# Second part of a fused kernel: its 36 token tiles in five chunks of 768 or 1024 tokens instead of six of 768

## The chip, the cores and the metric

One Trainium2 chip, one core. A time is what one execution takes on the device, in microseconds (us); a kernel's time is the median of its runs. The engines are named as the profile names them: PE (matrix products) with PEld (its weight loads), DVE (vector), ACT (scalar), POOL, and SP, which here issues every DMA.

## The reference

Three stages, all float32, on 8 sequences of 576 tokens with 512 features:

```
attention in blocks of 64 tokens, 8 heads of 64       -> x   (8, 576, 512)
h = relu(x @ w_in); gate = sigmoid(conv3(h))          -> x = (h * gate) @ w_out        (d_ff 1024)
u = x + real(fft over features of (fft over tokens))
un = (u - mean(u)) / sqrt(var(u) + 1e-6)
out = u + relu(un @ w_ch1) @ w_ch2                    w_ch1 (512, 2048), w_ch2 (2048, 512)
```

The last line, on 8 * 576 = 4608 tokens, is the second part of the kernel, and the change is in it.

## The kernel before

**Products in three passes.** Every float32 operand is split into a high and a low half: ACT copies it to the reduced format (L278), DVE subtracts that from the original (L279). A product then takes three matmuls: high by high, high by low, low by high.

**The second part** comes after the attention, the gated layer and the transforms, which end at about 630 us. The normalised rows u lie in DRAM as 36 tiles of 128 tokens. Both of its layers use a scheme of seven block products (B11, B21, T2, T1, T3, B22, T4) on sums of quarter blocks in place of eight: two row tiles that belong together (halves a = 0 and 1 of a chunk) are worked on at once, and the eighteen pairs of tiles are cut into NCH = 6 chunks of HT = 3 pairs, 768 tokens each.

**First layer, chunk by chunk.** `prep(c)` (L854) makes the operands of chunk c while chunk c - 1 is multiplied: per half it loads three tiles u (ring of three buffers), takes mean and variance (`stats`, L781: bn_stats, bn_aggr and a chain of small instructions once for the three), normalises (L801), transposes on PE (L806), copies from PSUM into buffers `raw` (L866), forms the sums (L818), and splits seven operands into the ring `sx` of seven pairs. A pair of `sx` comes free when the last group of the chunk before has used it. `gates` are products before which the loads of u are not issued: groups 3 and 5 for chunk 1, groups 1 and 3 for the later ones. `group(c, g)` (L884), eight per chunk, does the seven products of 128 hidden features by the chunk: six matmuls each (L904) whose moving operand has HTOK = 384 columns, HT tiles of one half. It then copies (L888), adds (L880), applies relu (L889) and stores four results m1, u2, u3, h21 to `h_scr` in DRAM (L929). m1, u2 and u3 have rings of two buffers each, h21 one.

**Beside it.** `load_tw` (L762) loads and splits the weight sums of layer one while chunk 0 runs and of layer two while the last chunk runs; `weight_sums_late` (L743) makes the sums of layer two, eight pieces, two in each of the chunks 1 to 4.

**Second layer.** `second(c, j)` (L933), one for each of the eighteen pairs, reads the four results back, splits them and multiplies (L971, 256 columns); this part is the same for any number of chunks but for where it finds its data.

**The order of the work** is written by a planner (`Plan.emit`, L151). Each operation has an engine, a cost and a due number `prio`; going through modelled time, the planner issues on each engine the ready operation with the lowest number. A chunk has 56 numbers, seven per group, whatever its width. A buffer's reuse, a gate and the landing of a DMA are dependencies in that model. The order so found is fixed: on the chip each engine, and SP's queue, takes its instructions in it. Among PSUM tiles, `x` is a ring of four in order and `o` four in any order.

Of the kernel before, what the change touches and what calls it, by code (L numbers as in the profile page):

```python
# [30 lines left out]
NCH2 = 18  # L31
FT2 = 16

NCH = 6
HT = 3
HTOK = 128 * HT
FG = 8

B11, B21, T2, T1, T3, T4, B22 = range(7)
CUTS = ((0, 1024), (1024, 1792))  # L40
# [182 lines left out]
def kernel(  # L223
# [19 lines left out]
    buf, op = plan.buf, plan.op  # L243
# [18 lines left out]

    u_scr = [[dram_buf(f"u_scr{i}{j}") for j in range(2)] for i in range(NCH2)]
    t_scr = [[dram_buf(f"t_scr{n}{g}", 1792) for g in range(FG)] for n in range(2)]
    first_scr = [dram_buf(f"first_scr{i}", 2 * HTOK) for i in range(7)]
    h_scr = [[dram_buf(f"h_scr{c}_{k}", FG * HTOK) for k in range(4)] for c in range(NCH)]

    def load(dst, src, nbytes, prio, r=(), after=()):
        return op("SP", 450, lambda: sp.dma_start(out=dst(), in_=src()), prio, r=r, w=[dst], after=after, nbytes=nbytes)
# [551 lines left out]
    first = []  # L821

    def stats_first(prios):
        first[:] = stats([lambda p, n=n: load_u(n, "w", "wide", 2, p - 4) for n in range(2 * HT)], "d", prios)

    def norm_first(j, prio):

        u = buf("w", "wide", 2, [128, 2, 512])
        for a in range(2):
            src = u_scr[(HT * a + j) // 2][(HT * a + j) % 2]  # L830
            op("SP", 450, lambda a=a, src=src: sp.dma_start(out=u()[:, a, :], in_=src()), prio - 6, r=[src], w=[u], nbytes=262144)
        for a in range(2):
            part = lambda t, a=a: t[:, a, :]
            tp = turned(u, *first, HT * a + j, prio, part)
            aop(512, lambda part=part, tp=tp: act.copy(out=part(u()), in_=tp().rearrange("p d n -> p (d n)")), prio, [tp], [u], True)
        s = buf("w", "wide", 2, [128, 4, 256])
        a11, a12, a21, a22 = (lambda a=a, k=k: u()[:, a, 256 * k:256 * k + 256] for a in range(2) for k in range(2))
        s1, s2, s3, s4 = (lambda k=k: s()[:, k, :] for k in range(4))
        tt(s1, a21, a22, ALU.add, 256, prio + 1, [u], [s])
        tt(s3, a11, a21, ALU.subtract, 256, prio + 1, [u], [s])  # L840
        tt(s2, s1, a11, ALU.subtract, 256, prio + 1, [u, s], [s])
        tt(s4, a12, s2, ALU.subtract, 256, prio + 1, [u, s], [s])
        two = lambda t: t.rearrange("p (d n) -> p d n", d=2)
        for i, x, b in ((A11, a11, u), (A12, a12, u), (A22, a22, u), (S1, s1, s), (S2, s2, s), (S3, s3, s), (S4, s4, s)):
            dst = first_scr[i]
            op("SP", 450, lambda x=x, dst=dst: sp.dma_start(out=two(dst())[:, :, 128 * j:128 * j + 128], in_=two(x())), prio + 1.5, r=[b], w=[dst], nbytes=131072)

    def prep_first(prio):
        for k, i in enumerate((A11, A12, S2, S1, S3, A22, S4)):
            s = buf("b", "raw", 6, [128, 2 * HTOK])  # L850
            load(s, first_scr[i], 1024 * HTOK, prio - 8 + k, r=[first_scr[i]])
            left((0, i), s, 2 * HTOK, prio + k, [128, 2 * HTOK], last_fold)

    def prep(c, prios, gates):  # L854

        raw = lambda: buf("b", "raw", 6, [128, 2, HTOK])
        blocks = []
        for a in range(2):
            ps = prios[HT * a:HT * a + HT]
            us = [load_u(2 * HT * c + HT * a + j, "e", "u", 3, p - 12, [gates[a]]) for j, p in enumerate(ps)]  # L860
            mv, r = stats(us, "b", ps)
            two = [raw(), raw()]
            for j, u in enumerate(us):
                tp = turned(u, mv, r, j, ps[-1])
                for k, b in enumerate(two):
                    aop(256, lambda j=j, k=k, b=b, tp=tp: act.copy(out=b()[:, :, 128 * j:128 * j + 128], in_=tp()[:, 2 * k:2 * k + 2, :]), ps[-1], [tp], [b], True)  # L866
            blocks += two
        a11, a12, a21, a22 = blocks
        s1, s2 = raw(), raw()
        n, p = 2 * HTOK, prios[-1]  # L870
        tt(s1, a21, a22, ALU.add, n, p, [a21, a22], [s1])
        tt(s2, s1, a11, ALU.subtract, n, p, [s1, a11], [s2])
        tt(a21, a11, a21, ALU.subtract, n, p, [a11, a21], [a21])
        for k, (i, x) in enumerate(((A11, a11), (A12, a12), (S2, s2), (S1, s1), (S3, a21), (A22, a22))):
            left((c, i), x, n, p + k, [128, 2, HTOK])
        tt(a12, a12, s2, ALU.subtract, n, p + 5, [a12, s2], [a12])
        left((c, S4), a12, n, p + 6, [128, 2, HTOK])

    def add_to(x, acc, n, prio, cut=lambda t: t):
        vop(n, lambda: dve.tensor_tensor(cut(x()), acc(), cut(x()), op=ALU.add), prio, [acc, x], [x])  # L880
# [1 line left out]


    def group(c, g, t):  # L884
        n = HTOK
        x1, x2 = (buf("ps", "x", 4, [128, n]) for _ in range(2))
        x3 = buf("ps", "o", 4, [128, n])
        copy = lambda x, acc, prio: aop(n, lambda: act.copy(out=x(), in_=acc()), prio, [acc], [x], True)  # L888
        relu = lambda x, acc, prio: aop(n, lambda: act.activation(out=x(), in_=acc(), func=ACT.Relu), prio, [acc], [x], acc is not x)  # L889

        def product(i, acc, prio, first=True):
            w, c0 = weight_of(0, g, i)
            x = sx[c, i]

            def unit():
                wh, wl, xh, xl = (a() for a in (*w, *x))
                if len(xh.shape) == 2:
                    xh, xl = (a.rearrange("p (a b) -> p a b", a=2) for a in (xh, xl))
                todo = []
                for k in range(2):  # L900
                    ws = slice(c0 + 128 * k, c0 + 128 * k + 128)
                    todo += [(wh[:, ws], xh[:, k, :]), (wh[:, ws], xl[:, k, :]), (wl[:, ws], xh[:, k, :])]
                for m, (a, b) in enumerate(todo):
                    pe.matmul(acc(), a, b, start=first and m == 0, stop=m == 5, skip_group_check=not first)  # L904

            return op("PE", mm_cost(n, passes=6), unit, prio, r=[*w, *x], w=[acc], after=() if c or g else last_d if i in (B11, B21) else last_s)

        m1, u2, u3, h21 = (buf("b", name, 1 if name == "h21" else 2, [128, n]) for name in ("m1", "u2", "u3", "h21"))
        begun = product(B11, x1, t)
        copy(m1, x1, t)  # L910
        product(B21, x3, t + 1)
        add_to(m1, x3, n, t + 1)
        relu(m1, m1, t + 1)
        product(T2, x1, t + 4, False)
        copy(u2, x1, t + 4)
        product(T1, x2, t + 5)
        product(T3, x1, t + 6, False)
        copy(u3, x1, t + 6)
        add_to(u3, x2, n, t + 6)
        relu(u3, u3, t + 6)  # L920
        product(T4, x1, t + 9, False)
        relu(h21, x1, t + 9)
        product(B22, x2, t + 10, False)
        add_to(u2, x2, n, t + 10)
        relu(u2, u2, t + 10)
        for k, (x, p) in enumerate(((m1, t + 2), (u2, t + 11), (h21, t + 10), (u3, t + 7))):
            dst = h_scr[c][k]
            to = lambda dst=dst: dst().rearrange("p (j g n) -> p j g n", j=HT, g=FG)[:, :, g, :]
            op("SP", 450, lambda x=x, to=to: sp.dma_start(out=to(), in_=x().rearrange("p (j n) -> p j n", j=HT)), p, r=[x], w=[dst], nbytes=512 * n)  # L929
        return begun  # L930


    def second(c, j, t, begin, end):  # L933
# [18 lines left out]
        tt(a12, a12, a11, ALU.subtract, n, t - 2, [a12, a11], [a12])  # L952
        make(S4, a12, 5)
        make(A22, a22, 6)
        us = [load_u(2 * HT * c + HT * a + j, "e", "u", 3, t - 4 + 3 * a) for a in range(2)]
        x1, x2, x3 = buf("ps", "x", 4, [128, 256]), buf("ps", "o", 4, [128, 256]), buf("ps", "o", 4, [128, 256])
        lo, hi = (lambda x: x[:, :256]), (lambda x: x[:, 256:])

# [14 lines left out]
            op("PE", mm_cost(256, passes=3 * len(gs)), unit, prio, r=[*x, *(a for w, _ in ws for a in w)], w=[acc])  # L973

        def store(a, prio, part=lambda x: x):
            m = 2 * HT * c + HT * a + j
            op("SP", 450, lambda: sp.dma_start(out=part(out[m // 2, :, m % 2, :]), in_=part(us[a]())), prio, r=[us[a]], nbytes=262144)

        accs = {B11: x1, B21: x3, T2: x1, T1: x2, T3: x1, B22: x2, T4: x1}
# [26 lines left out]
    for i in range(NH):  # L1006
# [4 lines left out]
        for f in range(FT):  # L1011
# [2 lines left out]
            while later and t + f >= FT + 9 * (FG - len(later)):  # L1014
                weight_sums(*later.pop(0), t + f + 8, [step])
            if t + f == 88:
                stats_first([88 + 2 * n for n in range(2 * HT)])
            if t + f in (103, 111, 119):
                norm_first((t + f - 103) // 8, t + f)
        if i == 0:  # L1020
# [36 lines left out]
    for c in range(NCH):  # L1057
        t = start + span * c
        begun = []
        for g in range(FG):  # L1060
            begun.append(group(c, g, t + 7 * g))
            if 1 <= c <= 4 and g in (0, 2):
                n = 2 * (c - 1) + g // 2
                weight_sums_late(n, rows(w_ch2)[n], t + 7 * g + 10)
        if c + 1 < NCH:
            prep(c + 1, [t + 7 * g for g in (2, 3, 4, 4, 5, 6)], [begun[g] for g in ((1, 3) if c else (3, 5))])
    t = start + span * NCH
    for g in range(FG):
        load_tw(1, g, [t - span + 7 * g + 8, t - span + 7 * g + 11])
    for c in range(NCH):  # L1070
        for j in range(HT):
            second(c, j, t + 7 * (HT * c + j), c + j == 0, c == NCH - 1 and j == HT - 1)

    with tc.manual_schedule():
        make_identity(nc, ident)
# [117 lines left out]
```

## Time and profile before

| | |
|---|---|
| runs, us | 1356.65, 1357.13, 1360.19; median 1357.13 |
| the profiled execution | 1356.65 us, its span 1356.6 us |
| PE busy | 1321.3 us (97%), 11376 matmuls |
| PEld, DVE, ACT, POOL busy | 1291.2 (95%), 1047.4 (77%), 802.3 (59%), 73.0 us (5%) |
| DMA | 206.5 MB, mean 152 GB/s |
| mean granted clock of PE | 0.996 of full speed |
| chain that ended last | PE 52% of the span: L904 25%, L971 26% |

Busy time of PE is the union of spans whose ends are modelled, so matmuls overlap in it: what one matmul takes in a stream is read from the distance of their starts, not from their duration. The page's 40 slices show PE at nine tenths or more in all but the first two. The second part is the stretch from 612 us to the end.

### The profile page before, as it was taken

How to read it: one execution, taken by the hardware profiler on the slowest of the kernel's cores; microseconds unless marked ns; L12 is line 12 of the kernel's file. 1: busy time of each engine (PE TensorE's matmuls, PEld its weight loads, DVE VectorE, ACT ScalarE, POOL GpSimd, SP SyncE). 2: the span in 40 equal slices, each digit the busy share in tenths (PEclk: the TensorE clock that was granted, in tenths of full speed). 3: DMA queues.
4: the chain of work that ended last, by engine and by line, in shares of the span. 5: the costliest groups of instructions: out<-in, count | busy, mean ns of one | idle time of the engine just before them, and what ended most of it. 6: DMA issues, size and time to landing. Idle time of an engine off the chain costs nothing.

```text
span 1356.6 us, 29701 instructions
## 1 busy us (share of the span) xinstructions
PE 1321.3 (97%) x11376; PEld 1291.2 (95%) x11376; DVE 1047.4 (77%) x2027; ACT 802.3 (59%) x2189; POOL 73.0 (5%) x195
## 2 busy tenths in 40 slices
PE   6899999999999999998999999999999999999999
PEld 4699999999999999997999999999999999999998
DVE  7999898889977686767776676765598777777773
ACT  6777675868677676655766665656763333333331
POOL 1101020101011110210000000000000000000000
PEclk9999999999999999999999999999999999999999
DMA  8523514232522132236856657669855554554441
GB/s 308 157 86 116 185 64 151 83 123 89 190 88 81 61 111 63 63 112 199 251 178 186 198 165 230 184 194 298 243 161 187 169 172 134 164 171 142 154 141 39
DMA packets 154573, 206.50 MB, mean 152 GB/s; under 512 B 11584, under 2 KB 103360, under 8 KB 154432
## 3 DMA queue, kind: packets, MB, share of 16 engines
q1 hardware_dynamic: 154432, 204.61, 48.0%
q8 instruction: 89, 1.46, 0.5%
q14 instruction: 52, 0.43, 0.1%
HBM read 130.51 MB, written 74.06 MB: 151 GB/s over the span
## 4 chain that ended last, share of the span: by engine, by line
PE 52%; DVE 1%; ACT 0%; issue 0%; DMA 0%; DVEq 0%; ACTq 0%
PE x L904 21%; PE x L971 15%; PE o L971 11%; PE o L904 4%; PE o L806 1%; DVE sxl L279 0%; DVE raw L818 0%; DMA h_scr<-u 0%; ACT th L278 0%; DVE u L880 0%; DVE tl L279 0%; ACT u L888 0%; PE o L673 0%; ACT u L889 0%; DVE u L700 0%
## 5 line engine op out<-in xcount | busy, mean ns | idle before, releaser
L278 ACT CAST sxh<-raw 128x1024 fp32r<-128x1024 f32 (+1 forms) x150 | 147.4, 990 | 187.8 <-PE o L971 83.4
L464 PE MATMUL o<-x,wih 128*128 128x320 f32 (+1 forms) x960 | 198.6, 300 | 1.6 <-DVE x L441 1.0
L279 DVE TENSOR_TENSOR sxl<-raw,sxh 128x1024 fp32r<-128x1024 f32 (+1 forms) x150 | 170.9, 1147 | 36.0 <-ACT sxh L278 35.9
L904 PE MATMUL x<-sxh,th 128*128 128x384 f32 x576 | 193.3, 336 | 2.0 <-ACT u L888 1.2
L904 PE MATMUL x<-sxh,tl 128*128 128x384 f32 x576 | 192.5, 334 | 0.0
L904 PE MATMUL x<-sxl,th 128*128 128x384 f32 x576 | 192.4, 334 | 0.0
L971 PE MATMUL x<-th,sxl 128*128 128x256 f32 x576 | 163.1, 283 | 0.5 <-DVE sxl L279 0.5
L971 PE MATMUL x<-th,sxh 128*128 128x256 f32 x576 | 163.1, 283 | 0.1
L971 PE MATMUL x<-tl,sxh 128*128 128x256 f32 x576 | 163.0, 283 | 0.0
L464 PEld LDWEIGHTS o<-x,wih 128*128 128x128 f32 x960 | 153.2, 188 | 3.9 <-DVE x L441 1.4
L481 DVE SCALAR_TENSOR_TENSOR cv<-h,cw,cv 128x255 f32<-128x255 f32 (+2 forms) x256 | 129.1, 515 | 32.0 <-ACT cv L495 23.9
L880 DVE TENSOR_TENSOR u<-x,u 128x384 f32<-128x384 f32 (+1 forms) x168 | 83.4, 497 | 86.3 <-ACT u L888 29.2
L532 PE MATMUL x<-gh,woh 128*128 128x322 f32 (+1 forms) x480 | 145.6, 303 | 0.0
L532 PE MATMUL x<-gh,wol 128*128 128x322 f32 (+1 forms) x480 | 142.4, 297 | 0.0
L532 PE MATMUL x<-gl,woh 128*128 128x322 f32 (+1 forms) x480 | 142.2, 296 | 0.1
L464 PE MATMUL o<-x,wil 128*128 128x320 f32 (+1 forms) x480 | 142.1, 296 | 0.0
L971 PE MATMUL o<-th,sxl 128*128 128x256 f32 x432 | 122.3, 283 | 0.0
L971 PE MATMUL o<-tl,sxh 128*128 128x256 f32 x432 | 122.3, 283 | 0.0
L971 PE MATMUL o<-th,sxh 128*128 128x256 f32 x432 | 122.2, 283 | 0.0
L971 PEld LDWEIGHTS x<-th,sxl 128*128 128x128 f32 x576 | 110.6, 192 | 0.7 <-DVE sxl L279 0.7
L971 PEld LDWEIGHTS x<-th,sxh 128*128 128x128 f32 x576 | 110.6, 192 | 0.5 <-ACT h L889 0.5
L904 PEld LDWEIGHTS x<-sxh,th 128*128 128x128 f32 x576 | 108.1, 188 | 2.6 <-ACT u L888 1.5
(286 smaller groups left out, 3216.6 us busy)
## 6 DMA issues: line engine op xcount, KB each, us to landing
raw<-h_scr SPq DMA_DIRECT2D x72, 512.0 KB, 4.4
h_scr<-u SPq DMA_DIRECT2D x96, 192.0 KB, 2.6
u<-u_scr SPq DMA_DIRECT2D x66, 256.0 KB, 4.2
qk<-in_qk_b SPq DMA_DIRECT2D x32, 320.0 KB, 3.5
h_scr<-m SPq DMA_DIRECT2D x48, 192.0 KB, 2.9
h_scr<-h SPq DMA_DIRECT2D x48, 192.0 KB, 3.0
out_y<-u SPq DMA_DIRECT2D x35, 256.0 KB, 2.4
wide<-in_w_ch SPq DMA_DIRECT2D x16, 512.0 KB, 4.0
```

Of the source, the lines that this page charges most:

```text
L278: aop(n, lambda: act.copy(out=cut(h()), in_=cut(src())), prio, [src], [h], psum, after=after)
L279: vop(n, lambda: dve.tensor_tensor(cut(l()), cut(src()), cut(h()).bitcast(F32), op=ALU.subtract), prio, [src, h], [l])
L464: pe.matmul(acc(), w[:, ws], x, start=k == 0, stop=k == 11)
L481: vop(hi - lo, lambda: dve.scalar_tensor_tensor(cv()[:, lo:hi], in0=h()[:, src:src + hi - lo], scalar=tap(k), in1=cv()[:, lo:hi], op0=ALU. ...
L532: pe.matmul(accs[d](), w[:, dsl], x, start=f == 0 and k == 0, stop=f == FT - 1 and k == 2)
L806: pe.transpose(tp()[:, d, :], cut(u())[:, 128 * d:128 * d + 128], ident)
L880: vop(n, lambda: dve.tensor_tensor(cut(x()), acc(), cut(x()), op=ALU.add), prio, [acc, x], [x])
L904: pe.matmul(acc(), a, b, start=first and m == 0, stop=m == 5, skip_group_check=not first)
L971: pe.matmul(acc(), a, b, start=first and m == 0 and gs[0] == 0, stop=gs[-1] == FG - 1 and m == len(todo) - 1, skip_group_check=not first)
```

## The change

The eighteen pairs are cut into five chunks of HT = (3, 4, 4, 3, 4) pairs: 768, 1024, 1024, 768, 1024 tokens. In the three chunks of four the first layer's matmuls have 512 columns. What follows from it: 

- `prep` takes the tiles of a half two at a time, so that `stats` runs for two (or one) tiles and not for three; the ring of u stays at three. All chunks after the first have their loads gated by groups 1 and 3.
- m1, u2 and u3 share one ring `h` of five buffers in place of three rings of two.
- B21 is ordered after B11 of the same group.
- `weight_sums_late` runs in groups 0, 2, 4 of chunks 1 and 2 and in groups 0, 2 of chunk 3.

```diff
-NCH = 6
-HT = 3
-HTOK = 128 * HT
+HT = (3, 4, 4, 3, 4)
+NCH = len(HT)
+TILE0 = tuple(2 * sum(HT[:c]) for c in range(NCH))
+FIRST = 128 * HT[0]
+LATE = tuple((c, g) for c, n in ((1, 3), (2, 3), (3, 2)) for g in range(0, 2 * n, 2))
...
     def prep(c, prios, gates):
-        raw = lambda: buf("b", "raw", 6, [128, 2, HTOK])
+        tok = 128 * HT[c]
+        raw = lambda: buf("b", "raw", 6, [128, 2, tok])
         for a in range(2):
-            ps = prios[HT * a:HT * a + HT]
-            us = [load_u(2 * HT * c + HT * a + j, "e", "u", 3, p - 12, [gates[a]]) for j, p in enumerate(ps)]
-            mv, r = stats(us, "b", ps)
+            ps = prios[HT[c] * a:HT[c] * a + HT[c]]
             two = [raw(), raw()]
-            for j, u in enumerate(us):
-                tp = turned(u, mv, r, j, ps[-1])
...
+            for j0 in range(0, HT[c], 2):
+                js = range(j0, min(j0 + 2, HT[c]))
+                us = [load_u(TILE0[c] + HT[c] * a + j, "e", "u", 3, ps[j] - 12, [gates[a]]) for j in js]
+                mv, r = stats(us, "b", ps[j0:js.stop])
+                for j, u in zip(js, us):
+                    tp = turned(u, mv, r, j - j0, ps[js.stop - 1])
...
     def group(c, g, t):
-        n = HTOK
+        n = 128 * HT[c]
...
-        m1, u2, u3, h21 = (buf("b", name, 1 if name == "h21" else 2, [128, n]) for name in ("m1", "u2", "u3", "h21"))
+        m1, u2, u3, h21 = (buf("b", *name, [128, n]) for name in (("h", 5), ("h", 5), ("h", 5), ("h21", 1)))
         begun = product(B11, x1, t)
         copy(m1, x1, t)
-        product(B21, x3, t + 1)
+        product(B21, x3, t + 1, after=[begun])
...
-            if 1 <= c <= 4 and g in (0, 2):
-                n = 2 * (c - 1) + g // 2
+            if (c, g) in LATE:
+                n = LATE.index((c, g))
                 weight_sums_late(n, rows(w_ch2)[n], t + 7 * g + 10)
         if c + 1 < NCH:
-            prep(c + 1, [t + 7 * g for g in (2, 3, 4, 4, 5, 6)], [begun[g] for g in ((1, 3) if c else (3, 5))])
+            prep(c + 1, [t + 7 * g for g in ((2, 2, 3, 3, 4, 4, 5, 6) if HT[c + 1] == 4 else (2, 3, 4, 4, 5, 6))], [begun[g] for g in (1, 3)])
```

In `norm_first`, `prep_first`, `second`, the loads and the stores HT becomes HT[0] or HT[c], and tile numbers start from TILE0[c]; nothing else differs there.

## Rows read from the trace of the kernel before

**Rows 1.** Busy time by stretch: us, five engines (instructions), PE clock, DMA share, GB/s.
```profile
605.00:640.00 35.00, 29.29 (x179) 26.71 (x179) 27.81 (x53) 20.83 (x46) 1.55 (x8) 0.95 0.51 154
640.00:687.00 47.00, 47.00 (x282) 46.87 (x281) 35.87 (x70) 34.84 (x71) 0.00 (x0) 1.00 0.76 233
687.00:870.00 183.00, 183.00 (x1083) 182.71 (x1083) 128.81 (x266) 111.19 (x245) 0.00 (x0) 1.00 0.64 192
870.00:931.00 61.00, 61.00 (x363) 60.90 (x362) 42.04 (x88) 37.42 (x83) 0.00 (x0) 1.00 0.72 214
931.00:982.00 51.00, 51.00 (x296) 51.00 (x295) 26.75 (x37) 33.91 (x64) 0.00 (x0) 1.00 0.87 275
982.00:996.00 14.00, 13.64 (x93) 13.11 (x91) 13.51 (x15) 10.31 (x16) 0.00 (x0) 1.00 0.55 158
996.00:1356.60 360.60, 357.13 (x2974) 356.93 (x2974) 273.05 (x319) 128.01 (x125) 0.00 (x0) 1.00 0.47 148
```

**Rows 2.** PE's waits from 605 to 1000: us in total, times, longest (seven lines).
```profile
PE x L904 <- ACT u L888: 1.2, 1, 1.2
...
PE o L904 <- DVE sxl L279: 0.7, 1, 0.7
PE x L971 <- DVE sxl L279: 0.5, 1, 0.5
```

**Rows 3.** Chain that ended last, in order of time: start us, us, what.
```profile
641.13 6.24 PE x L904 x36
...
693.74 21.85 PE x L904 x126
...
1002.01 2.88 PE x L971 x24
```

**Rows 4.** Timeline of PE, 322 columns: first and last of 29 matmuls in a row.
```profile
594.72 0.31 PE L532 MATMUL x<-gl,woh 128*128 128x322 f32 x1
...
598.88 0.32 PE L532 MATMUL x<-gh,wol 128*128 128x322 f32 x1
```

**Rows 5.** Line L904: count, ns min/median/max, first and last start (three such pairs).
```profile
L904 PE MATMUL x<-sxh,th x576: 334/334/445, 612.4 to 994.9; 128*128 128x384 f32 x192
...
L904 PE MATMUL o<-sxh,th x96: 334/334/689, 613.5 to 958.5; 128*128 128x384 f32 x96
```

**Rows 6.** DVE by line, 632 to 687: count, busy us, mean ns, idle before it.
```profile
L787 DVE BATCH_NORM_STATS2 st<-u 128x6 f32<-128x512 f32 x6 | 4.0, 673 | 0.0
L818 DVE TENSOR_TENSOR raw<-raw 128x768 f32<-128x768 f32 x4 | 3.7, 955 | 0.0
L279 DVE TENSOR_TENSOR sxl<-raw,sxh 128x768 fp32r<-128x768 f32 x4 | 3.6, 953 | 0.0
L801 DVE TENSOR_SCALAR u<-u,mv,r 128x512 f32<-128x512 f32 x6 | 2.9, 542 | 0.0
...
L792 DVE RECIPROCAL r<-r 128x3 f32<-128x3 f32 x2 | 0.3, 173 | 0.7 <-ACT r L791 0.7
```

**Rows 7.** Timeline of DVE: operand splits of chunk 1; a sum of 1024 columns.
```profile
678.21 1.82 DVE L279 TENSOR_TENSOR sxl<-raw,sxh 128x768 fp32r<-128x768 f32 x2
...
686.06 1.82 DVE L279 TENSOR_TENSOR sxl<-raw,sxh 128x768 fp32r<-128x768 f32 x2
...
988.49 1.22 DVE L818 TENSOR_TENSOR ts<-raw 128x1024 f32<-128x1024 f32 x1
```

**Rows 8.** Timeline of ACT: relu of one group's u2, copy of m1 two groups on.
```profile
720.66 0.53 ACT L889 ACTIVATE u<-u 128x384 f32<-128x384 f32 x1 [1.09 <-DVE u L880]
...
724.23 0.48 ACT L888 COPY m<-x 128x384 f32<-128x384 f32 x1 [0.56 <-PE x L904]
```

**Rows 9.** DMAs on h_scr, stores and loads together: time from issue to landing.
```profile
DMA to landing us min/median/max: 2.3/3.5/8.6
```

**Rows 10.** SP's queue, waits from 632 to 1000: us in total, times, longest.
```profile
SPq L269 <- PE o L806: 11.9, 7, 2.8
```

More of the change, by code (lines that the diff above doesn't have):

```diff
@@ L264 @@
     t_scr = [[dram_buf(f"t_scr{n}{g}", 1792) for g in range(FG)] for n in range(2)]
-    first_scr = [dram_buf(f"first_scr{i}", 2 * HTOK) for i in range(7)]
-    h_scr = [[dram_buf(f"h_scr{c}_{k}", FG * HTOK) for k in range(4)] for c in range(NCH)]
+    first_scr = [dram_buf(f"first_scr{i}", 2 * FIRST) for i in range(7)]
+    h_scr = [[dram_buf(f"h_scr{c}_{k}", FG * 128 * HT[c]) for k in range(4)] for c in range(NCH)]
     def load(dst, src, nbytes, prio, r=(), after=()):
@@ L823, in stats_first @@
     def stats_first(prios):
-        first[:] = stats([lambda p, n=n: load_u(n, "w", "wide", 2, p - 4) for n in range(2 * HT)], "d", prios)
+        first[:] = stats([lambda p, n=n: load_u(n, "w", "wide", 2, p - 4) for n in range(2 * HT[0])], "d", prios)
     def norm_first(j, prio):
@@ L829, in norm_first @@
         for a in range(2):
-            src = u_scr[(HT * a + j) // 2][(HT * a + j) % 2]
+            src = u_scr[(HT[0] * a + j) // 2][(HT[0] * a + j) % 2]
             op("SP", 450, lambda a=a, src=src: sp.dma_start(out=u()[:, a, :], in_=src()), prio - 6, r=[src], w=[u], nbytes=262144)
@@ L833, in norm_first @@
             part = lambda t, a=a: t[:, a, :]
-            tp = turned(u, *first, HT * a + j, prio, part)
+            tp = turned(u, *first, HT[0] * a + j, prio, part)
             aop(512, lambda part=part, tp=tp: act.copy(out=part(u()), in_=tp().rearrange("p d n -> p (d n)")), prio, [tp], [u], True)
@@ L849, in prep_first @@
         for k, i in enumerate((A11, A12, S2, S1, S3, A22, S4)):
-            s = buf("b", "raw", 6, [128, 2 * HTOK])
-            load(s, first_scr[i], 1024 * HTOK, prio - 8 + k, r=[first_scr[i]])
-            left((0, i), s, 2 * HTOK, prio + k, [128, 2 * HTOK], last_fold)
+            s = buf("b", "raw", 6, [128, 2 * FIRST])
+            load(s, first_scr[i], 1024 * FIRST, prio - 8 + k, r=[first_scr[i]])
+            left((0, i), s, 2 * FIRST, prio + k, [128, 2 * FIRST], last_fold)
     def prep(c, prios, gates):
-        raw = lambda: buf("b", "raw", 6, [128, 2, HTOK])
+        tok = 128 * HT[c]
+        raw = lambda: buf("b", "raw", 6, [128, 2, tok])
         blocks = []
         for a in range(2):
-            ps = prios[HT * a:HT * a + HT]
-            us = [load_u(2 * HT * c + HT * a + j, "e", "u", 3, p - 12, [gates[a]]) for j, p in enumerate(ps)]
-            mv, r = stats(us, "b", ps)
+            ps = prios[HT[c] * a:HT[c] * a + HT[c]]
             two = [raw(), raw()]
-            for j, u in enumerate(us):
-                tp = turned(u, mv, r, j, ps[-1])
-                for k, b in enumerate(two):
-                    aop(256, lambda j=j, k=k, b=b, tp=tp: act.copy(out=b()[:, :, 128 * j:128 * j + 128], in_=tp()[:, 2 * k:2 * k + 2, :]), ps[-1], [tp], [b], True)
+            for j0 in range(0, HT[c], 2):
[4 more added lines that the diff above has]
+                    tp = turned(u, mv, r, j - j0, ps[js.stop - 1])
+                    for k, b in enumerate(two):
+                        aop(256, lambda j=j, k=k, b=b, tp=tp: act.copy(out=b()[:, :, 128 * j:128 * j + 128], in_=tp()[:, 2 * k:2 * k + 2, :]), ps[js.stop - 1], [tp], [b], True)
             blocks += two
@@ L869, in prep @@
         s1, s2 = raw(), raw()
-        n, p = 2 * HTOK, prios[-1]
+        n, p = 2 * tok, prios[-1]
         tt(s1, a21, a22, ALU.add, n, p, [a21, a22], [s1])
@@ L874, in prep @@
         for k, (i, x) in enumerate(((A11, a11), (A12, a12), (S2, s2), (S1, s1), (S3, a21), (A22, a22))):
-            left((c, i), x, n, p + k, [128, 2, HTOK])
+            left((c, i), x, n, p + k, [128, 2, tok])
         tt(a12, a12, s2, ALU.subtract, n, p + 5, [a12, s2], [a12])
-        left((c, S4), a12, n, p + 6, [128, 2, HTOK])
+        left((c, S4), a12, n, p + 6, [128, 2, tok])
     def add_to(x, acc, n, prio, cut=lambda t: t):
@@ L889, in group, with product @@
         relu = lambda x, acc, prio: aop(n, lambda: act.activation(out=x(), in_=acc(), func=ACT.Relu), prio, [acc], [x], acc is not x)
-        def product(i, acc, prio, first=True):
+        def product(i, acc, prio, first=True, after=()):
             w, c0 = weight_of(0, g, i)
@@ L904, in unit @@
                     pe.matmul(acc(), a, b, start=first and m == 0, stop=m == 5, skip_group_check=not first)
-            return op("PE", mm_cost(n, passes=6), unit, prio, r=[*w, *x], w=[acc], after=() if c or g else last_d if i in (B11, B21) else last_s)
-        m1, u2, u3, h21 = (buf("b", name, 1 if name == "h21" else 2, [128, n]) for name in ("m1", "u2", "u3", "h21"))
+            return op("PE", mm_cost(n, passes=6), unit, prio, r=[*w, *x], w=[acc], after=[*((last_d if i in (B11, B21) else last_s) if c + g == 0 else ()), *after])
+        m1, u2, u3, h21 = (buf("b", *name, [128, n]) for name in (("h", 5), ("h", 5), ("h", 5), ("h21", 1)))
         begun = product(B11, x1, t)
         copy(m1, x1, t)
-        product(B21, x3, t + 1)
+        product(B21, x3, t + 1, after=[begun])
         add_to(m1, x3, n, t + 1)
@@ L927, in group @@
             dst = h_scr[c][k]
-            to = lambda dst=dst: dst().rearrange("p (j g n) -> p j g n", j=HT, g=FG)[:, :, g, :]
-            op("SP", 450, lambda x=x, to=to: sp.dma_start(out=to(), in_=x().rearrange("p (j n) -> p j n", j=HT)), p, r=[x], w=[dst], nbytes=512 * n)
+            to = lambda dst=dst: dst().rearrange("p (j g n) -> p j g n", j=HT[c], g=FG)[:, :, g, :]
+            op("SP", 450, lambda x=x, to=to: sp.dma_start(out=to(), in_=x().rearrange("p (j n) -> p j n", j=HT[c])), p, r=[x], w=[dst], nbytes=512 * n)
         return begun
@@ L954, in second @@
         make(A22, a22, 6)
-        us = [load_u(2 * HT * c + HT * a + j, "e", "u", 3, t - 4 + 3 * a) for a in range(2)]
+        us = [load_u(TILE0[c] + HT[c] * a + j, "e", "u", 3, t - 4 + 3 * a) for a in range(2)]
         x1, x2, x3 = buf("ps", "x", 4, [128, 256]), buf("ps", "o", 4, [128, 256]), buf("ps", "o", 4, [128, 256])
@@ L975, in store @@
         def store(a, prio, part=lambda x: x):
-            m = 2 * HT * c + HT * a + j
+            m = TILE0[c] + HT[c] * a + j
             op("SP", 450, lambda: sp.dma_start(out=part(out[m // 2, :, m % 2, :]), in_=part(us[a]())), prio, r=[us[a]], nbytes=262144)
@@ L1016 @@
             if t + f == 88:
-                stats_first([88 + 2 * n for n in range(2 * HT)])
+                stats_first([88 + 2 * n for n in range(2 * HT[0])])
             if t + f in (103, 111, 119):
@@ L1070 @@
     for c in range(NCH):
-        for j in range(HT):
-            second(c, j, t + 7 * (HT * c + j), c + j == 0, c == NCH - 1 and j == HT - 1)
+        for j in range(HT[c]):
+            second(c, j, t + 7 * (TILE0[c] // 2 + j), c + j == 0, c == NCH - 1 and j == HT[c] - 1)
     with tc.manual_schedule():
```

## The prediction

> **What bounds the kernel now.** I read the busy time by stretch first. From 640 us to 982 us PE is busy without a break while DVE stands at 69 to 76% where chunks are prepared and at 52% in the last chunk, and DMA at 0.64 to 0.87 [rows 1]. PE's waits confirm it: of all that PE waited for between 605 and 1000 us there are seven entries, 6.2 us in all, the largest 1.2 us; those on the first layer lie before 640 us and the last, 0.5 us, at the handover to the second layer [rows 2]. So the first layer is a stream of matmuls, and only the number of matmuls and what one takes set its length.
>
> What one takes is read from the chain of waits: 36 in 6.24 us and 126 in 21.85 us, 173.3 ns each at 384 columns; 24 in 2.88 us, 120.0 ns each at 256 columns [rows 3]. The 128 columns between them cost 53.3 ns, which is 0.417 ns per column, one column per cycle at 2.4 GHz, the level that goes with the granted clock of 1.00 there [rows 1]. What is left over is the same for both: 173.3 - 160.0 = 13.3 and 120.0 - 106.7 = 13.3 ns. A third width agrees: at 322 columns, 28 steps in 4.16 us, 148.6 ns, against 134.2 + 13.3 = 147.5 [rows 4]. So a matmul pays 13.3 ns once, whatever its width between 256 and 384.
>
> **The change, part by part.**
>
> *Fewer, wider matmuls.* Before there are 3 x (576 + 96) = 2016 of them [rows 5], 336 per chunk: 2016 x 173.3 ns = 349.4 us. After there are two chunks of 384 columns, 672 x 173.3 = 116.5 us, and three of 512, 1008 x (213.3 + 13.3 = 226.7) = 228.5 us; together 345.0 us. The columns are the same, 336 matmuls are gone, 336 x 13.3 ns = **4.48 us saved**, all of it on the path, because PE is the path. No row shows 512 columns. If the overhead grew with the width as 173.3 / 384 does, a matmul would take 231.1 ns and nothing would be saved; if it vanished, 213.3 ns, and the saving would be 17.9 us. Three widths on one straight line make me take 226.7.
>
> The Trainium skill (TensorE: Matmul & The Clock Gate, "Wait — 56ns, not 53.3ns?") puts the fixed cost of a matmul at about 2.5 ns at full clock. By that rule the 336 that go would be worth 0.84 us and the change would not be measurable. The rows above contradict it here with 13.3 ns, and I go by the rows.
>
> *Preparation of chunk 1 in chunk 0.* Eight tiles in place of six, in the same 58 us of products. DVE has in addition two tiles' bn_stats and normalisation, 2 x (0.67 + 0.54) = 2.4 us [rows 6] with some 0.4 us of bn_aggr; two more chains of small instructions, six at about 0.17 us each, 2.0 us [rows 6]; four sums and about four splits that grow from 0.95 to 1.22 us, 2.2 us [rows 6, 7]. Together 7.0 us. From 640 to 687 us DVE is idle for 11.1 us [rows 1], and the loads are released two groups earlier, 2 x 7.3 us by 42 matmuls of 173.3 ns. So I cost it at nothing, hidden beside PE. If that cover is gone: the split that chunk 1 needs third ends at 687.9 us [rows 7], and its product comes some 2.7 us later by the order B11, B21, two products left over from the group before, T2; 7.0 - 2.7 = 4.3 us would then stand on the path. The same holds for chunk 4, which is prepared in the 384-wide chunk 3: of the stretch from 687 to 870 us DVE has 70% [rows 1], or 42.9 us of 61; with the same 7.0 us that is 82%. I take 0, with 4.3 us at either place as the upper end. A gain there is excluded: PE waits for nothing at these borders now.
>
> *The middle chunks.* In 76 us of products DVE prepares eight tiles (or six) and three pieces of late weights in place of two. Per 61 us it now does 42.9 us, two pieces in it [rows 1]; with 7.0 more, 26 us of 76 are left for the third piece. Nothing.
>
> *The ring of five.* m1 of a group now takes the buffer that u2 had two groups before, and so waits for the landing of u2's store; before, it waited for m1's own. In the steady order u2's relu ends at 720.66 + 0.53 = 721.19 us and m1 is copied at 724.23 us, 3.04 us later [rows 8]. A store lands after 2.3 us at best, 3.5 in the middle, 8.6 at worst (loads are in this figure too) [rows 9]. ACT's copy is then late by some half a microsecond, and what stands behind it in ACT's queue (relus, operand casts) with it. PE feels it only at T2, which adds onto the same PSUM tile and comes three products later: 3 x 1.04 - 0.48 = 2.6 us of room, so a landing is hidden up to 5.7 us at 384 columns and, all times 226.7/173.3, about 7.4 us at 512. I take +0.4 us for a few late landings; bounds 0 and 8.6 - 5.7 = 2.9 us for each landing at its worst.
>
> *SP's queue.* A half of four tiles has a ring of three, so its fourth load waits for the first transposes. Such waits exist now, seven of 2.8 us or less [rows 10]; there will be about twice as many, and the stores of results are queued behind them. They add to the landing times above and are priced there.
>
> *Border to the second layer.* DVE is busy for 13.51 of 14.00 us from 982 to 996, and PE loses 0.36 us of busy time there [rows 1], with a wait of 0.5 us [rows 2]. The last group now takes 9.5 in place of 7.3 us for the same operands of `second`, so DVE has 2.2 us more. I take -0.4 us, between -0.9 and +0.5 (the order is new).
>
> *Entry.* The waits before 640 us, with a clock of 0.95 [rows 1], come from the end of the transforms and from chunk 0, whose width stays. I take 0, between -2 and +2: PE is idle there for 5.7 us, and a new order can shift a third of it either way. The second layer, 360.6 us with PE at 99% [rows 1], has the same instructions: 0.
>
> Sum: -4.48 + 0.4 - 0.4 = -4.5 us. The profiled execution took 1356.65 us with a span of 1356.6, so nothing lies around it, and it is 0.5 us under the median: 1352.2 us against it, **1352.6 us** as a median.
>
> **The rivals.**
>
> *A: the preparation does not fit.* At one of the two borders from a narrow chunk to a wide one the 4.3 us above stand on the path; with both, 8.6. For it: DVE and ACT go back and forth in the chain of `stats`, so idle time is not all usable, and from 982 to 996 us a DVE at 96% did make PE wait. Against it: 11.1 us of idle DVE and the earlier loads. One border gives 1357.1 - 4.5 + 4.3 = 1356.9 us, no change.
>
> *B: the ring of five stops PE.* Place: T2 in the 384-wide chunk 0, where six of the eight weight loads run beside the loads of u and DMA is at 0.76 [rows 1]. Price: 2.9 us for each landing at its worst. It decides from the third on: 3 x 2.9 = 8.7 us is more than the 4.5 saved and the 4.1 that can be told. With four, 1357.1 - 4.5 + 11.6 = 1364.2 us, slower. For it: the worst landing is real [rows 9], and ACT in that chunk is at 74% [rows 1], so lost time is not made up quickly. Against it: the planner knows the ring and an estimate of the landing, and puts other products first; the median landing is covered.
>
> *C: width costs more than the line says.* A 512-wide matmul takes up to 231.1 ns, so the change does not do what it says: between 1352.6 and 1357.1, say 1355.8 us. For it: no row at 512. Against it: three widths on one line. The Trainium skill's fixed cost of 2.5 ns (page and section as above) would end in the same place, at 1357.1 - 0.8 = 1356.3 us; with 13.3 ns in the rows I give it 0.01 of C's chance.
>
> **How the numbers follow.** What can be told from no change for this kernel is about 0.3%, 4.1 us, so faster means under 1353.0 us. My forecast 0.53 (its own range 1350.3 to 1353.0: the entry and the border can add to the gain, and more than that is not there to be won), A 0.26 with the small new waits that leave 1353 to 1357 us, B 0.15, C 0.06. The forecast is near the edge: half a microsecond of new waits turns it into no change. Faster 0.53; same A and C, 0.32; slower B, 0.15. The range from 1350.2 to 1360.5 leaves out about 0.05 below and, of B, 0.12 above.
>
> **What would show it.** In the profile after: 1680 matmuls on L904, 504 x 2 of them with 512 columns at 226.7 ns from start to start (C is wrong, or right at 231); PE without waits at the ends of the first and the fourth chunk (else A, by a wait of L904 on a split or on ACT); no wait of L904 that ends with ACT's copy of m1 behind a store of u (else B); the second layer as long as before, 360 us. I am wrong if the time is above 1353.0 us, and wrong in kind if the stream after 640 us has gaps of more than 2 us.

## The result, and the profile after

The changed kernel takes 1367.79 us (median of four runs, 1365.5 to 1368.25) against 1357.82 us for the kernel before (1356.65 to 1360.19): 1.007 times as long, 95% interval 1.0057 to 1.0082. It is slower, by some 10 us. The profiled execution took 1368.25 us with a span of 1366.5 us, so 1.75 us lie around a span. The prediction had taken the profiled execution of before to be as long as its span, 1356.65 us; by the same 1.75 us it was about 1358.4.

Busy time by stretch of the changed kernel; the columns are those of [rows 1]:

```profile
613.00:641.00 28.00, 22.98 (x124) 21.14 (x123) 19.83 (x36) 14.23 (x30) 0.00 (x0) 0.88 0.58 171
641.00:694.00 53.00, 51.22 (x296) 49.09 (x296) 44.67 (x92) 38.68 (x79) 0.00 (x0) 1.00 0.75 232
694.00:774.00 80.00, 79.18 (x367) 66.03 (x368) 57.46 (x114) 45.29 (x87) 0.00 (x0) 1.00 0.64 192
774.00:853.00 79.00, 78.76 (x362) 65.23 (x361) 54.56 (x113) 45.88 (x86) 0.00 (x0) 1.00 0.61 183
853.00:912.00 59.00, 58.39 (x343) 57.12 (x342) 40.99 (x95) 33.97 (x80) 0.00 (x0) 1.00 0.70 209
912.00:950.00 38.00, 34.09 (x146) 27.63 (x145) 21.82 (x29) 21.79 (x36) 0.00 (x0) 0.96 0.81 272
950.00:1007.00 57.00, 57.00 (x280) 48.37 (x279) 34.51 (x39) 39.93 (x58) 0.00 (x0) 1.00 0.67 198
1007.00:1366.00 359.00, 356.15 (x2968) 355.94 (x2967) 269.57 (x315) 124.70 (x121) 0.00 (x0) 1.00 0.47 148
```

Where PE had been busy without a break from 640 to 982 us, it now has holes, above all from 641 to 694 us (the first chunk and the border to the second) and from 912 to 950 us (the start of the fifth chunk). After the handover, from 1007 us on, nothing is new.

PE's waits from 640 to 1010 us (us in total, times, longest), where before only 0.5 us stood [rows 2]:

```profile
PE x L909 <- ACT h L893: 7.0, 8, 2.4
PE x L909 <- DVE h L885: 0.8, 1, 0.8
```

L909 is L904 of before, L893 is the copy of a product from PSUM into m1, u2 or u3, and h is their common ring. PE waits for ACT's copy.

The matmuls themselves did what was forecast. Two pieces of the chain that ended last, one of a wide and one of a narrow chunk:

```profile
894.38 6.25 PE x L909 x36
...
960.82 9.52 PE x L909 x42
```

42 in 9.52 us are 226.7 ns each at 512 columns, the value that the line through [rows 3, 4] gives, and 36 in 6.25 us are 173.6 ns at 384. Their number, one of three such pairs (3 x 560 = 1680), is in the answer on the line:

```profile
L909 PE MATMUL x<-sxh,th x480: 331/389/689, 613.8 to 1005.2; 128*128 128x512 f32 x97, 128*128 128x384 f32 x63
...
L909 PE MATMUL o<-sxh,th x80: 333/389/476, 614.9 to 989.9; 128*128 128x512 f32 x48, 128*128 128x384 f32 x32
```

So the 4.48 us were saved, and more than that was lost. For each kernel below I add up, matmul by matmul, the distance from its start to the start of the next, less what it takes in a full stream, (columns / 2.4 + 13.3) ns, or 109 ns for a transpose: this is what PE lost. From 640 to 1010 us the kernel before loses 1.4 us and the changed one 13.6: 2.6 up to 690, 4.0 up to 910, 7.0 up to 950. The difference, 12.2 us, less 4.5, is 7.7 us; another 1.4 us is lost from 599 to 640 us, at the entry, where losses lie between 11.4 and 14.1 us in all kernels here. Of the 9.9 us between the two spans that leaves 0.8, of which 0.6 lie ahead of 599 us.

**One hole from close by.** Timeline of PE in the changed kernel (start us, us, instruction, idle before it and what ended it):

```profile
917.38 0.34 PE L909 MATMUL x<-sxh,tl 128*128 128x384 f32 x1
920.15 0.69 PE L909 MATMUL x<-sxh,th 128*128 128x384 f32 x1 [2.43 <-ACT h L893]
920.64 0.52 PE L909 MATMUL x<-sxl,th 128*128 128x384 f32 x1
920.96 0.52 PE L909 MATMUL x<-sxh,tl 128*128 128x384 f32 x1
```

and of ACT at the same time:

```profile
915.46 0.52 ACT L894 ACTIVATE h<-h 128x384 f32<-128x384 f32 x1 [1.53 <-DVE h L885]
915.89 0.46 ACT L893 COPY h<-x 128x384 f32<-128x384 f32 x1
917.32 0.53 ACT L894 ACTIVATE h<-h 128x384 f32<-128x384 f32 x1 [0.97 <-DVE h L885]
917.75 1.98 ACT L280 CAST sxh<-raw 128x1024 fp32r<-128x1024 f32 x2
919.63 0.47 ACT L893 COPY h<-x 128x384 f32<-128x384 f32 x1
```

The copy at 919.63 us, for which PE waits, did not wait for anything itself: ACT was busy. Two casts for the next chunk's operands, 1.98 us, stand ahead of it in ACT's order. And the hole costs more than its 2.43 us: after it the matmuls start 320 ns apart in place of 173 (920.64 to 920.96), the lower of the two clock levels, until 923.5 us, which loses another 1.6 us; the stretch has a granted clock of 0.96.

Not every wait for a copy is of this kind. Of the 7.0 us, three waits (2.4, 1.2 and 0.2 us, together 3.9) end with a copy that stood behind casts, and one of 0.7 us with a copy that stood behind a relu. In the four others, of 0.6 to 0.7 us each, the copy starts as soon as its product is done: there PE's own order has no other product between the one that is copied and the one that adds onto it.

### The profile page after: what moved, and what is told of

It is laid out like the page before. It is cut to its first block, busy times and chain, and to the rows that moved or that the text cites. A ratio compares the mean times of both kernels' runs of the same rounds, so it can differ in the third digit from the quotient of the medians.

```text
span 1366.5 us, 28865 instructions
## 1 busy us (share of the span) xinstructions
PE 1324.7 (97%) x11040; PEld 1250.6 (92%) x11040; DVE 1049.0 (77%) x2028; ACT 796.0 (58%) x2132; POOL 73.6 (5%) x195
## 4 chain that ended last, share of the span: by engine, by line
PE 50%; ACT 1%; DVE 1%; DMA 0%; issue 0%; SPq 0%; ACTq 0%
PE x L909 19%; PE x L976 15%; PE o L976 11%; PE o L909 3%; PE o L808 1%; ACT sxh L280 0%; ACT h L893 0%; DVE h L885 0%; DMA t_scr<-ts 0%; DVE sxl L281 0%; DVE raw L820 0%; DMA h_scr<-h 0%; ACT h L894 0%; DVE u L803 0%; SPq L934 0%
## 5 line engine op out<-in xcount | busy, mean ns | idle before, releaser
L909 PE MATMUL x<-sxh,th 128*128 128x512 f32 (+1 forms) x480 | 180.0, 375 | 8.7 <-ACT h L893 7.0
L909 PE MATMUL x<-sxh,tl 128*128 128x512 f32 (+1 forms) x480 | 177.4, 370 | 0.0
L909 PE MATMUL x<-sxl,th 128*128 128x512 f32 (+1 forms) x480 | 177.3, 369 | 0.0
L909 PEld LDWEIGHTS x<-sxh,th 128*128 128x128 f32 x480 | 90.9, 189 | 25.1 <-ACT h L893 11.4
L976 PEld LDWEIGHTS x<-tl,sxh 128*128 128x128 f32 x576 | 110.6, 192 | 0.0
```

Source lines behind the costliest of these rows:

```text
L976: pe.matmul(acc(), a, b, start=first and m == 0 and gs[0] == 0, stop=gs[-1] == FG - 1 and m == len(todo) - 1, skip_group_check=not first)
```

## The experiments

The theories: **R**, the ring of five, either by waits on the chip for stores that land late (**W**, rival B of the prediction) or by the order that the planner writes for such a ring (**O**); **P**, the preparation of a four-tile chunk beside a narrow one (rival A). Times are medians; each ratio is against the kernel before, run on the same chip in the same rounds, where its medians lie between 1357.8 and 1358.4 us.

| | time, us | ratio, 95% interval | PE loss 640 to 1010, us |
|---|---|---|---|
| before | 1357.8 | 1 | 1.4 |
| after | 1367.8 | 1.0070 (1.0057 to 1.0082) | 13.6 |
| e1 own rings | 1359.1 | 1.0004 (0.9994 to 1.0013) | 8.0 |
| e2 order kept | 1367.0 | 1.0058 (1.0043 to 1.0073) | 16.1 |
| e3 order of own | 1359.7 | 1.0010 (1.0000 to 1.0020) | 6.9 |
| e4 late weights early | 1364.2 | 1.0041 (1.0026 to 1.0056) | 14.5 |
| e5 ring of five in six chunks | 1364.8 | 1.0053 (1.0039 to 1.0066) | 8.0 |
| e6 B21 after B11 in six chunks | 1363.9 | 1.0045 (1.0031 to 1.0058) | 6.9 |
| e7 own rings, B21 free | 1359.9 | 1.0020 (1.0010 to 1.0031) | 8.0 |
| e8 the same, chunks 3, 3, 4, 4, 4 | 1355.2 | 0.9982 (0.9974 to 0.9991) | 3.3 |
| e9 chunks 3, 3, 4, 4, 4 alone | 1365.9 | 1.0053 (1.0040 to 1.0067) | 14.6 |
| e10 e8, weights early | 1353.6 | 0.9969 (0.9958 to 0.9980) | 1.8 |

**e1 to e3: the ring, its waits and its order.** Five buffers can also be dealt out by name:

```diff
-        ... for name in (("h", 5), ("h", 5), ("h", 5), ("h21", 1)))
+        ... for name in (("m1", 2), ("u2", 2), ("u3", 1), ("h21", 1)))
```

The planner and the memory are separate here: a Buf tells the planner its ring, and its tile is allocated when the instruction is written out. So e2 plans with the ring and allocates by name, e3 the other way round:

```diff
 class Buf:
+        self.placed = (tag, bufs)
...
-                self.shape, self.dtype, tag=self.tag, name=self.tag, bufs=self.bufs
+                self.shape, self.dtype, tag=self.placed[0], name=self.placed[0], bufs=self.placed[1]
 def group(c, g, t):                                   # e2; in e3 by name above, placed = ("h", 5)
+        for x, name in ((m1, ("m1", 2)), (u2, ("u2", 2)), (u3, ("u3", 1))):
+            x.placed = name
```

> The changed kernel with its five result buffers dealt out by name (m1 two, u2 two, u3 one) in place of one ring of five; memory, chunks and all else as in the changed kernel. Theory R (the ring of five costs the time): of the 13.5 us that PE loses between 640 and 950 us most comes back, 1356 to 1361 us against 1367.8. Theory P (preparing a four-tile chunk beside a narrow one overloads ACT and DVE at the two borders): the losses of about 3.9 us before the second chunk and 7 us around the fifth stay, 1365 to 1368 us.

> The changed kernel with the order of all instructions as it is, planned for the ring of five, but the buffers themselves dealt out by name as in e1, so that no copy into m1 or u2 waits for the store of another result. If the ring costs time on the chip through stores that land late (theory W, as rival B had it), this gains as much as e1: below 1361 us. If it costs through the order that the planner writes for it (theory O), nothing changes: 1366 to 1369 us. Theory P: nothing changes either.

> The other way round: the order planned for buffers by name (that of e1), but the buffers in one ring of five, so that the waits for landings are there and the order is e1's. Theory O: as e1, within 2 us. Theory W: as the changed kernel or slower, 1366 us or more, since the order takes no account of these waits. Theory P: as the changed kernel.

The four kernels make a square. With the order of the ring: 1367.8 us in the ring (after), 1367.0 with buffers by name (e2). With the order by name: 1359.7 us in the ring (e3), 1359.1 by name (e1). The order makes 8 us, the buffers less than one. PE's losses from 599 to 1010 us, the entry included, say the same: 27.6 and 27.4 us with the order of the ring, 19.7 and 19.4 with that by name. (From 640 us alone e2 loses more than the changed kernel, in part because the granted clock is at its lower level for 6.8 us there and not for 3.4.) PE's waits from 640 to 950 us in e2:

```profile
PE x L910 <- ACT u L894: 6.7, 7, 2.4
PE x L910 <- DVE u L886: 0.8, 1, 0.8
PE x L910 <- ACT m L894: 0.7, 1, 0.7
```

Here the buffers have names (the profile leaves numbers out, so u is u2 or u3). Of 7.4 us that PE waits for copies, 0.7 are for m1, on which T2 waits; 6.7 are for u2 and u3, on which T3 and T4 wait. The hole of 2.43 us is a T3 that waits for u2.

In e3:

```profile
PE x L910 <- ACT h L894: 0.8, 2, 0.6
PE x L910 <- DVE h L886: 0.6, 1, 0.6
```

And in e1, from 640 to 1010 us:

```profile
PE o L976 <- DVE sxl L281: 2.0, 1, 2.0
PE x L909 <- ACT u L893: 1.2, 1, 1.2
PE x L976 <- DVE u L885: 0.9, 1, 0.9
PE x L909 <- DVE u L885: 0.6, 1, 0.6
```

The hole of 2.43 us stands in e2 as it did in the changed kernel. Two lines of ACT and one of PE, in order of time:

```profile
914.51 1.98 ACT L281 CAST sxh<-raw 128x1024 fp32r<-128x1024 f32 x2
916.40 0.47 ACT L894 COPY u<-x 128x384 f32<-128x384 f32 x1
```

```profile
916.92 0.69 PE L910 MATMUL x<-sxh,th 128*128 128x384 f32 x1 [2.43 <-ACT u L894]
```

e2 has no ring of five in memory and has the holes; e3 has the ring and not the holes. W is wrong, O is right, and P, which expected e1 at 1365 us or more, is at most a small part. What is shown is that the order costs the time. Why the planner writes it is read from its code and was not tried, and the code has two candidates. Its model holds a copy back until the store that had the buffer before has landed (L128 and L190 of the changed kernel). And it doesn't let a buffer be written before the one ahead of it in its ring (L131), so a shared ring ties the copies to the order m1, u2, u3, group after group. In e2's trace the copies follow that order throughout, two of u between one of m1 and the next; in e1's trace another number stands there in 19 of 40 groups. No run tells the two apart.

**e4: two pieces of late weights out of the narrow chunk.**

```diff
-LATE = tuple((c, g) for c, n in ((1, 3), (2, 3), (3, 2)) for g in range(0, 2 * n, 2))
+LATE = tuple((c, g) for c, n in ((1, 4), (2, 4)) for g in range(0, 2 * n, 2))
```

> The changed kernel with the eight pieces of late weights in groups 0, 2, 4, 6 of chunks 1 and 2, none in chunk 3, where chunk 4 of four tiles is prepared. This takes two pieces, some 9 us of DVE work and 2 us of ACT work, out of the narrow chunk. Theory P: the loss of about 7 us between 912 and 950 us goes down to 2 or less, 1361 to 1364 us. Theory R: within 1.5 us of the changed kernel's 1367.8.

The time went down by 3.6 us, to the edge of what P gave and out of what R gave, but not where P said: PE's loss from 910 to 950 us is 7.0 us in both, though in other holes (1.7 and 2.3 us in place of 2.4). The prediction of P for that place failed, and so did that of R for the time. Where e4's gain lies is open. The trace can't show it: it is of the slowest of e4's four executions, 1366.87 us, only 1.4 us under the profiled one of the changed kernel (its loss from 640 to 1010 us is no smaller, and from 599 to 640 it is 11.9 against 14.0 us).

**e5 and e6: single edits in the kernel before.**

```diff
-        ... (buf("b", name, 1 if name == "h21" else 2, [128, n]) for name in ("m1", "u2", "u3", "h21"))
+        ... (buf("b", *name, [128, n]) for name in (("h", 5), ("h", 5), ("h", 5), ("h21", 1)))     # e5
-        product(B21, x3, t + 1)
+        product(B21, x3, t + 1, after=[begun])                                                      # e6
```

> The kernel before, six chunks of 768, with one thing of the change: m1, u2, u3 in one ring of five. Theory O (the order planned for a ring of five has PE wait for ACT's copies): slower, by 3 to 8 us, 1361 to 1366 us, with waits of the first layer's products on ACT's copy behind 640 us, where there were none. Theory P (wide chunks beside narrow ones): no change, 1357 to 1359 us.

> The kernel before with one other thing of the change: B21 ordered after B11 of its group. It takes from the planner a product that it can put in while the PSUM ring x is full. If this order is part of the loss (theory O2): slower by 1 to 5 us, 1359 to 1363 us. If the ring alone makes it: 1357 to 1359 us.

Each makes the six-chunk kernel 6 to 7 us slower by itself, without any wide chunk; e6 is 0.9 us above what O2 gave. (e5 also takes one buffer away, five in place of six. That alone is not what costs in five chunks, where e1 has five too.) PE's waits from 640 to 1010 us in e5:

```profile
PE x L904 <- ACT h L888: 4.8, 6, 1.7
```

and in e6:

```profile
PE x L904 <- ACT u L888: 2.2, 4, 0.8
PE x L904 <- DVE u L880: 1.0, 2, 0.7
PE x L904 <- ACT h L889: 0.4, 1, 0.4
PE o L806 <- DVE u L801: 0.2, 1, 0.2
```

Mostly the same wait in both: a product that adds onto a PSUM tile, for the copy out of it. e5's losses are 6.6 us over those of before and its time 7.0, e6's 5.5 and 6.1. The two excesses add up to 12.1 us, what the changed kernel has, 12.2; that is no proof that both are in it, since they don't come off one by one, as e7 shows.

**e7 and e8: the rest.** e7 is e1 with `product(B21, x3, t + 1)` as before; e8 is e7 with HT = (3, 3, 4, 4, 4).

> The changed kernel with buffers by name (as e1) and B21 no longer ordered after B11. By O2 the 3 us that e1 still loses from 641 to 694 us go, 1355 to 1358 us. If that loss is of the preparation of a four-tile chunk beside the first narrow chunk (theory P in its small form), it stays: within 1.5 us of e1's 1359.1.

> As e7, with the chunks in the order 3, 3, 4, 4, 4 tiles, so that the first chunk prepares a narrow one. Small P: the loss from 641 to 694 us goes to under 1 us and the time to 1352 to 1356 us, faster than the kernel before. Otherwise as e7. All theories of width: 336 matmuls fewer than before, 4.5 us, wherever PE has no waits.

e7 is no better than e1 in time, and O2 failed there: the order of B21 costs in six chunks and, once the ring's order is gone, nothing that the time shows in five. PE's losses are less plain. From 640 to 950 us they go from 4.6 in e1 to 3.0 in e7 (2.0 of it up to 690 us), but at the handover from 3.4 to 5.1: there, 1.5 us after a wait of 1.87 us, the granted clock was 0.50 from 997.2 to 1000.6 us, which it was not in e1. e8 moves the first border between a narrow and a wide chunk away from the entry, where the splits of the first layer's weights share DVE with the preparation: the loss up to 690 us falls from 2.0 to 0.4. That is what P in its small form said, 1.6 us of the 4.3 that rival A priced; that the shared DVE is the reason is argued, not shown. The time of e8 lies in small P's range by more than its reason, though: the loss at the handover falls too, from 5.1 to 2.2 us, and the clock stays at its upper level there. e8 is faster than the kernel before, by 2.6 us of medians; from losses and matmuls, 3.3 - 1.4 - 4.5 = -2.6 us.

**e9: the order of the chunks alone.**

> The changed kernel with nothing but the chunks in the order 3, 3, 4, 4, 4: ring of five and B21 after B11 as in the change. Theory O: the ring's order still costs most of its time, 1362 to 1366 us. If the order of the chunks is the whole matter: as e8, under 1357 us.

As O has it: 1365.9 us, at the upper end, with PE's waits from 640 to 1010 us led by the same one:

```profile
PE x L909 <- ACT h L893: 6.3, 9, 1.9
```

While the ring and B21 stay, the order of the chunks gives nothing that is clear of the intervals (1.0053 against 1.0070).

**e10: the handover.** In `load_tw(1, ...)` both due numbers of each weight piece are four lower. Ahead of the second layer's first operands DVE had this order in e8:

```profile
983.32 0.96 DVE L281 TENSOR_TENSOR tl<-ts,th 128x768 fp32r<-128x768 f32 x1 [0.29 <-ACT th L280]
984.20 1.22 DVE L820 TENSOR_TENSOR ts<-raw 128x1024 f32<-128x1024 f32 x1
...
989.77 1.21 DVE L820 TENSOR_TENSOR raw<-raw 128x1024 f32<-128x1024 f32 x1
991.07 0.69 DVE L885 TENSOR_TENSOR u<-x,u 128x512 f32<-128x512 f32 x1
991.67 2.35 DVE L281 TENSOR_TENSOR sxl<-raw,sxh 128x1024 fp32r<-128x1024 f32 x2
```

> e8 with the loads and splits of the second layer's weights due four numbers (four products) earlier in the last chunk, so that the last splits no longer stand between the sums for the second layer's first operands on DVE. In e8 PE loses 2.2 us there. If that is DVE's work at the handover: 1 us or more less, 1353 to 1355 us. If it is the landing of the data: no change, 1355.

The splits of the last operands begin at 988.60 in place of 991.67 us:

```profile
980.98 2.08 DVE L281 TENSOR_TENSOR tl<-ts,th 128x1024 fp32r<-128x1024 f32 x2
982.98 1.22 DVE L820 TENSOR_TENSOR ts<-raw 128x1024 f32<-128x1024 f32 x1
...
988.60 2.35 DVE L281 TENSOR_TENSOR sxl<-raw,sxh 128x1024 fp32r<-128x1024 f32 x2
```

PE's waits from 640 to 1010 us in e8 are these two,

```profile
PE x L976 <- DVE sxl L281: 1.1, 1, 1.1
PE x L976 <- ACT sxh L280: 0.3, 1, 0.3
```

and in e10 this one:

```profile
PE x L976 <- DVE sxl L281: 0.2, 1, 0.2
```

With 1353.6 us e10 is the fastest kernel of this study, 0.9969 of the kernel before (0.9958 to 0.9980): 4.2 us by the ratio, against 4.48 of matmuls saved and 0.4 us lost more than before. e8 and e10 were not run in the same rounds, so their 1.6 us between them rest on their ratios and on the trace.

## Why the prediction was wrong

- **Fewer, wider matmuls, -4.48 us: right.** 1680 of them, 226.7 ns at 512 columns; rival C falls. The fixed cost of 13.3 ns holds from 256 to 512 columns. e10 shows the gain in the time.
- **The ring of five, +0.4 us: this step failed**, in its mechanism and in its place. That PE waits for ACT's copy was right. But I let it wait at T2 alone, three products and 2.6 us after the copy of m1, and T2 has 0.7 of the 7.4 us of such waits in e2. T3 and T4 add onto the same PSUM tile behind the copies of u2 and u3, and I left them out; by the due numbers only T1 stands between T2 and T3, an estimate of 1.04 - 0.48 = 0.6 us of room. And I priced landings that come late on the chip, and argued against rival B that the planner knows the ring and would put other work first. It did, and that is the cost: it wrote casts ahead of the copies, for 3.9 of PE's 7.0 us, and it wrote PE's products so that one follows straight on the product whose copy it needs, for 2.5. In time the ring costs 1367.8 - 1359.1 = 8.7 us (after and e1); in PE's losses 5.6 from 640 us and 8.2 from 599 us. Which rule of the planner makes that order is open. The landings were much as before, 2.3, 3.6 and 9.3 us at least, in the middle and at most, against [rows 9], and e3 shows that they cost less than a microsecond.
- **B21 after B11: left out.** I listed the edit and gave it no cost. In six chunks it costs 6.1 us (e6). The reason to ask was in sight: the planner used that freedom (in the trace of before, B21 of several groups comes ahead of its turn), PE had no waits [rows 2], and an added dependency takes some of it away. But what it takes need not be missed: in five chunks with buffers by name the time is no better without it (e7).
- **Preparation beside the narrow chunk, 0: too low, but small.** 1.6 us at the first border by e7 and e8, and 0.5 us left around the fifth chunk in e1, not the 4.3 of rival A at either. Moving late weights away (e4) didn't lessen the loss at the fifth chunk, so DVE's share, 76% before [rows 1] and 84% after (44.67 of 53 us), was the wrong measure of it.
- **Late weights, nothing: open.** With the two pieces out of the narrow chunk the kernel is 3.6 us faster (e4), and no run shows where.
- **Handover, -0.4 us: right in sign for this kernel, by luck.** The loss there goes from 1.1 to 0.0 us, a gain past the bound of 0.9; with PE less delayed the loss is 3.4 us in e1 and 5.1 in e7, and 0.8 in e10.
- **Entry, 0: +1.4 us**, inside its bound of 2; the granted clock is 0.88 there, against 0.95 before [rows 1].
- **The clock.** I costed a hole at its length. After the one of 2.43 us the clock stayed at its lower level for 3.4 us, which lost 1.6 us more.
- **Around the span, 0: 1.75 us**, as said with the result.

Rival B had the sign and, with 1364.2 us, a time 3.6 us under the measured one, at a chance of 0.15. That was luck: it had worst landings at T2, and neither is what costs. Its chance and its time were too small because I took a planner's foresight as a safeguard. Its estimates decide the order, and the order was the cost.

## What to carry to other kernels

Where the order of the instructions is computed, a dependency can cost by what it does to the order, even if hardly anything waits for it on the chip: keep the order and take away the dependency, and the other way round, to tell the two apart. Price every edit that adds a dependency or shortens a ring, above all where the bound engine has no waits, since then any wait that the new order brings is a loss. And price it at every place that waits for a copy, the nearest first. See what a shared ring ties together, which result waits for which buffer and in what order they must be used: the same five buffers, planned by name, gave 8 us.

## What the runs showed of the hardware

After a wait of PE of 2.43 us the granted clock was at its lower level: the next matmuls start 320 ns apart at 384 columns, against 173, from 920.15 to 923.5 us. Waits of 0.6 to 1.2 us at other places of the same stream left the clock alone: at 384 columns the first matmul after them takes some 280 ns from start to start, and from the second on the distance is 168 to 178 ns. Between these lengths the length does not decide. The clock fell after waits of 2.3 us (e4, from 946.7 to 950.1 us), 1.9 us (e9, from 755.0 to 758.4) and 1.87 us (e7, from 997.2 to 1000.6), some 1.5 us after the wait had ended; after a wait of 2.00 us in e1 and in e3, and of 1.7 us in e5, it stayed up.

In a full stream a matmul takes, from start to start, 120.0 ns at 256 columns, 173.3 at 384 and 226.7 at 512: one straight line with 13.3 ns on top.
